# Grouping the first loads of a fused S5 + SwiGLU kernel: twelve transfers in place of fifteen

## The chip, the cores and the metric

The kernel runs on one core of a Trainium2 chip. The metric is the device time of one execution in microseconds (us). Before the change it is 178.52 us, the median of three runs (178.37 to 178.71).

## The reference

A layer norm without gain feeds two branches that are added to the input: a diagonal complex state-space layer (S5) over 2048 tokens, and a SwiGLU feed-forward layer. Width D is 512, the state 512, the hidden width F 1376, everything in bfloat16.

```python
x = A_x                                   # [1, 2048, 512]
xn = _layernorm(x, axis=-1)
return x + _A_ref(xn, ...) + _B_ref(xn, B_w_gate, B_w_up, B_w_down)

def _A_ref(x, ...):                       # S5
    dt = jnp.exp(log_dt)
    Lam_bar = jnp.exp(dt * Lam)
    B_bar = ((Lam_bar - 1.0) / Lam)[:, None] * Bmat
    Bu = jnp.einsum("bld,pd->blp", x + 0j, B_bar)
    # h[t] = Lam_bar * h[t-1] + Bu[t], for t in range(2048)
    return 2.0 * jnp.einsum("blp,dp->bld", hseq, Cmat).real + x * Dskip[None, None, :]

def _B_ref(x, w_gate, w_up, w_down):      # SwiGLU
    return (silu(x @ w_gate) * (x @ w_up)) @ w_down
```

## The kernel before

The 2048 tokens are 16 tiles of 128, and four tiles make a chunk of 512. Most work goes chunk by chunk: B's projection of the normed tokens (`bproj_chunk`, line 380), the rotation and the scans of the recurrence on VectorE (lines 390 to 436), gate and up with their product (`gateup_chunk`, lines 455 to 474), and the output (`out_chunk`), which adds the feed-forward part (line 598) and the state part (line 611) in one PSUM bank. All the order is written out by hand: engines run their instructions in the order of the program, and a backlog of VectorE steps is pumped out between groups of matmuls.

The head is what the change touches. The matrices gate and up arrive row block by row block: row k is the 128 rows of the weight matrix that meet the k-th 128 columns of x, cut to the first 1024 of the 1376 columns (256 KB, `load_row`, line 117). The remaining 352 columns of each come as one transfer into `w_end` (line 113). x comes as tile 0 (SyncE's queue, line 123), tile 1 (ScalarE's queue, line 125), tiles 2 and 3 (lines 131 and 133) and then chunk 1 in one (line 141). SyncE (SP) issues its transfers in the order of the program; at most eight are under way, since each of eight semaphores serves every eighth transfer, and an issue waits for the landing of the transfer that had its semaphore before. A transfer's consumer waits for the whole transfer.

TensorE begins with dummy matmuls (line 668), transposes x of tiles 0 and 1 as soon as they are there (line 230), takes the mean out by a matmul (line 238), and then runs the weight rows in the order in which they arrive, `row_mm` (line 487): up's rows 0 to 3, gate's rows 0 to 2, and gate's row 3, each row with four matmuls (two tiles times two halves of the 1024 columns) into four PSUM banks. Between gate's rows 2 and 3 it transposes tile 2, which VectorE has centered by then:

```python
    row_mm(1, 0)
    pp = prm_transpose()
    ln_stats(2)
    center(2)
    ln_rstd(2, 3)
    ln_stats(3)
    ln_rstd(3, 4)
    prm_copy(pp)
    exp_pool(dt_t[:], ldt)
    for k in range(1, SW):
        row_mm(1, k)
    t2 = bank()
    for k in range(KD):
        cT_mm(t2, xc[:, 2, :], k, k == 0, k == KD - 1)
```

`ln_stats` (lines 182 and 183) are VectorE's statistics, `center` line 219, `ln_rstd` a small addition on VectorE (line 191) and a power on GpSimd (line 192). Tile 3 and then tiles 0 to 2 are normed (line 200) and turned by a DMA transpose (`xT0_dma`, line 251), behind which SP's queue has the transposes of B (line 145). Much later, after chunk 1's gate and up, SP copies A_x of the first three chunks into the output (line 856), and GpSimd adds the results to it with accumulating DMAs (line 618 and line 584).

Of the kernel before, what the change touches and what calls it, by code (L numbers as in the profile page):

```python
# [23 lines left out]
def kernel(  # L24
# [17 lines left out]
    nc = tc.nc  # L42
# [4 lines left out]
    CW = 512  # L47
    HW = CW // 2
    NT = L // 128
    NCH = L // CW  # L50
    TPC = CW // 128
    KD = D // 128
# [27 lines left out]
    x_v = A_x[0].rearrange("(n p) d -> p n d", p=128)  # L80
    out_v = out[0].rearrange("(n p) d -> p n d", p=128)
    wg_v = B_w_gate.rearrange("(k p) f -> p k f", p=128)
    wu_v = B_w_up.rearrange("(k p) f -> p k f", p=128)


    xall = const.tile([128, NT, D], BF16, name="xall")
# [3 lines left out]
    FE = fgroups[-1][0] * 128  # L90
    wg01 = const.tile([128, KD, FE], BF16, name="wg01")
    wu01 = const.tile([128, KD, FE], BF16, name="wu01")
# [18 lines left out]
    def load_w1(q, tiles, view, gi):  # L111
        a, b = fgroups[gi]
        q.dma_start(out=tiles[gi][:, :, :], in_=view[:, :, a * 128:F if gi == len(fgroups) - 1 else b * 128])


    def load_row(q, t, view, k):
        q.dma_start(out=t[:, k, :], in_=view[:, k, 0:FE])

    HK = KD // 2
    ident = const.tile([128, 128], BF16, name="ident")  # L120
# [3 lines left out]
    nc.vector.memset(xall[:, 1, 0:2], 0.0)  # L124
    nc.scalar.dma_start(out=xall[:, 1, :], in_=x_v[:, 1, :])
    nc.scalar.preload_act_table_set("silu_and_others")
    for k in range(KD):
        load_row(nc.sync, wu01, wu_v, k)
    for k in range(HK):
        load_row(nc.sync, wg01, wg_v, k)  # L130
    nc.sync.dma_start(out=xall[:, 2, :], in_=x_v[:, 2, :])
    load_row(nc.sync, wg01, wg_v, HK)
    nc.sync.dma_start(out=xall[:, 3, :], in_=x_v[:, 3, :])
    load_row(nc.sync, wg01, wg_v, HK + 1)
    load_w1(nc.sync, wg_g, wg_v, 2)
    load_w1(nc.sync, wu_g, wu_v, 2)
    prm_rows = const.tile([128, 128], BF16, name="prm_rows")
# [649 lines left out]
    def bproj_chunk(c):  # L787
        need(f"ln{c}")
        for part in range(2):
            for q in range(NQ):  # L790
                bproj_tile(c, part, q)
                pump(BP)
                multiply(0 if q else 1)
# [27 lines left out]
    def queue_ssm(c):  # L821
        fwd, back = ssm_ops(c)
        queue(f"ssm{c}", fwd + back)
# [28 lines left out]
    gateup_chunk(1)  # L852
    nc.gpsimd.dma_start(out=dsk_bc[:], in_=A_Dskip.partition_broadcast(128))
    bproj_chunk(2)
    for a in range(0, (NCH - 1) * CW, CW):
        nc.sync.dma_start(out=out[0, a:a + CW, :], in_=A_x[0, a:a + CW, :])
    queue_ssm(2)
    out_chunk(0)
    gateup_chunk(2)
# [45 lines left out]
```

## Time and profile before

| what | value |
|---|---|
| median of three runs | 178.52 us (178.37 to 178.71) |
| the profiled execution | 177.87 us |
| its span, first to last instruction | 175.8 us |
| TensorE busy | 171.4 us, 97% |
| VectorE busy | 156.9 us, 89% |
| ScalarE busy | 102.0 us, 58% |
| bytes moved by DMA | 17.88 MB, mean 102 GB/s |
| TensorE's granted clock | 0.999 |

Times in a profile's lines are microseconds from the span's start, unless marked ns. In the timeline a line has the start, the time that it took, the engine, the line of the program, the operation, and what it writes from what it reads; "x4" says that four of a kind in a row are one entry. PE is TensorE's matmuls, PEld its weight loads, DVE VectorE, ACT ScalarE, POOL GpSimd, and SPq are instructions of SP's queue, for a DMA the issue alone. In the list of DMAs the last number is the median time from issue to landing. The chain that ended last is followed back from the last instruction, at each step to what released it.

### The profile page before, as it was taken

Reading aid. Unit: us, or ns where it says so; the run is one execution under the profiler, and the core shown is the slowest. Engines: PE = TensorE matmul, PEld = TensorE weight load, DVE = VectorE, ACT = ScalarE, POOL = GpSimd, SP = SyncE. Lnnn points to the kernel's source line nnn. Section 1 sums busy time; section 2 is a strip of 40 time slices with the busy share of each in tenths; the row PEclk is TensorE's granted clock in tenths of the full one; section 3 lists DMA queues with packets and bytes.
Section 4 is the critical chain, followed back from the end, with each engine's and each line's share of the span. In section 5 each row is a group of like instructions: output and inputs, shape, how many; then the busy total and the mean of one; then the engine's idle time right before and its main releaser. Section 6 shows DMA issues by size and latency. Waiting matters only on the chain.

```text
span 175.8 us, 2365 instructions
## 1 busy us (share of the span) xinstructions
PE 171.4 (97%) x847; PEld 82.6 (47%) x863; DVE 156.9 (89%) x259; ACT 102.0 (58%) x188; POOL 28.1 (16%) x39
## 2 busy tenths in 40 slices
PE   8999999999999999999999999999999999999993
PEld 4544446464444444446444444446444444444542
DVE  3776999999999999999999999999999998699542
ACT  3379498793997685236598660024666653990100
POOL 5244110032000000044300000025000000522500
PEclk9999999999999999999999999999999999999999
DMA  5998929999999300047016000007200000696921
GB/s 184 344 350 83 245 48 205 285 191 300 161 218 306 112 4 0 0 38 82 2 34 119 0 0 0 0 0 87 36 15 17 0 4 0 87 175 96 117 66 60
DMA packets 34043, 17.88 MB, mean 102 GB/s; under 512 B 24896, under 2 KB 32928, under 8 KB 33984
## 3 DMA queue, kind: packets, MB, share of 16 engines
q1 hardware_dynamic: 30288, 14.22, 34.1%
q0 software_dynamic: 3456, 3.28, 14.4%
q10 hardware_dynamic: 288, 0.23, 0.4%
q8 instruction: 7, 0.11, 0.3%
q14 instruction: 4, 0.03, 0.1%
HBM read 8.03 MB, written 5.24 MB: 75 GB/s over the span
## 4 chain that ended last, share of the span: by engine, by line
PE 96%; DMA 1%; issue 1%; DVE 0%
PE ps L455 29%; PE ps L598 22%; PE ps L611 16%; PE ps L380 16%; PE ps L487 8%; PE ps L541 3%; PE ps L771 2%; DMA xall<-in_A_x_dram 1%; PE ps L230 1%; PE ps L238 0%; DVE xall L614 0%; PE ps L271 0%
## 5 line engine op out<-in xcount | busy, mean ns | idle before, releaser
L598 PE MATMUL ps<-wd_sb,guT 128*128 128x512 bf16 (+4 forms) x184 | 38.7, 366 | 0.2
L422 DVE TENSOR_TENSOR_SCAN g<-r_t,car,u 128x512 bf16<-128x512 f32 x24 | 29.1, 1264 | 0.0
L611 PE MATMUL ps<-CF,wt 128*128 128x512 bf16 (+2 forms) x134 | 28.4, 366 | 0.1
L380 PE MATMUL ps<-xnT,BT 128*128 128x512 bf16 x125 | 28.1, 379 | 0.2
L598 PEld LDWEIGHTS <-guT 128*128 128x128 bf16 (+1 forms) x187 | 17.9, 98 | 20.5
L455 PE MATMUL ps<-xnT,wu 128*128 128x512 bf16 x95 | 24.6, 379 | 0.2
L455 PE MATMUL ps<-xnT,wg 128*128 128x512 bf16 x91 | 23.9, 379 | 0.1
L618 POOL DMA_DIRECT2D out_dram<-res x12 | 10.5, 1043 | 77.3 <-ACT res L617 72.1
L469 ACT ACTIVATE guT<-ps 128x512 bf16<-128x512 f32 x30 | 18.3, 609 | 4.8 <-PE ps L455 4.5
L470 ACT CAST u<-ps 128x512 bf16<-128x512 f32 x30 | 17.9, 596 | 4.6 <-PE ps L455 4.5
L382 ACT CAST u<-ps 128x512 bf16<-128x512 f32 x32 | 17.5, 597 | 4.8 <-PE ps L380 3.3
L611 PEld LDWEIGHTS <-wt 128*128 128x128 bf16 x136 | 13.0, 98 | 14.7
L380 PEld LDWEIGHTS <-BT 128*128 128x128 bf16 x128 | 12.5, 98 | 14.8
L617 ACT CAST res<-ps 128x512 bf16<-128x512 f32 x12 | 6.8, 583 | 21.0 <-PE ps L611 21.0
L572 ACT ACTIVATE xr<-xall,nb,rstd 128x512 bf16<-128x512 bf16 x16 | 11.8, 805 | 9.1 <-DVE xall L580 4.9
L455 PEld LDWEIGHTS <-wu 128*128 128x128 bf16 x96 | 9.4, 98 | 11.3
L455 PEld LDWEIGHTS <-wg 128*128 128x128 bf16 x96 | 9.3, 98 | 10.6
L192 POOL TENSOR_TENSOR rstd<-ve,neg_half 128x1 f32<-128x1 f32 (+1 forms) x7 | 7.6, 1079 | 29.4 <-DVE ve L191 29.0
L455 PE MATMUL ps<-xnT,w_end 128*128 128x512 bf16 x48 | 10.9, 379 | 0.0
L182 DVE BATCH_NORM_STATS2 stats<-xall 128x6 f32<-128x512 bf16 x16 | 10.8, 675 | 0.0
L474 DVE TENSOR_TENSOR guT<-guT,u 128x1024 bf16<-128x1024 bf16 x15 | 10.0, 675 | 0.0
L390 DVE TENSOR_TENSOR pm<-g,c 128x2048 bf16<-128x2048 bf16 x8 | 9.8, 1220 | 0.1
(120 smaller groups left out, 207.8 us busy)
## 6 DMA issues: line engine op xcount, KB each, us to landing
out_dram<-in_A_x_dram SPq DMA_DIRECT2D x3, 512.0 KB, 5.3
out_dram<-res POOLq DMA_DIRECT2D x12, 128.0 KB, 3.1
out_dram<-xall POOLq DMA_DIRECT2D x3, 512.0 KB, 6.0
wd_sb<-in_B_w_down_dram SPq DMA_DIRECT2D x1, 1280.0 KB, 8.2
wu<-in_B_w_up_dram SPq DMA_DIRECT2D x4, 256.0 KB, 3.8
wg<-in_B_w_gate_dram SPq DMA_DIRECT2D x4, 256.0 KB, 4.8
xall<-in_A_x_dram SPq DMA_DIRECT2D x1, 1024.0 KB, 7.0
xall<-in_A_x_dram SPq DMA_DIRECT2D x1, 512.0 KB, 6.1
```

The costliest lines, as they stand in the source:

```text
L182: nc.vector.bn_stats(out=stats[:, n, 0, :], in_=xall[:, n, :])
L380: nc.tensor.matmul(ps[:] if c else by_k(ps[:]), lhsT=BT[:, part, k, q * 128:(q + 1) * 128], rhs=xnT[:, c, k, :] if c else xnT0[:, k], star ...
L382: nc.scalar.copy(out=u_tiles[c][:, part, q, :], in_=ps[:])
L422: V.tensor_tensor_scan(out=g()[:, part, q, :], data0=r_t[:, q:q + 1].to_broadcast([128, CW]), data1=u_tiles[c][:, part, q, :], initial=ini ...
L455: nc.tensor.matmul(ps[:fs, lo:hi], lhsT=wslice(groups, fi, k), rhs=xnT[:, c, k, lo:hi], start=(k == 0), stop=(k == KD - 1))
L469: nc.scalar.activation(out=guT[:fs, fi, :], in_=psg[:fs], func=ACT.Silu)
L470: nc.scalar.copy(out=u_pair[c][:fs, fi % 2, :], in_=psu[:fs])
L487: nc.tensor.matmul(ps[:, 0:(b - a) * 128], lhsT=tokens(i, k), rhs=groups[gi][:, k, 0:(b - a) * 128], start=(k == 0), stop=(k == KD - 1))
L572: nc.scalar.activation(out=box["xr"][:], in_=xall[:, n, :], func=ACT.Identity, scale=rstd[:, n:n + 1], bias=nb[:, n:n + 1])
L598: nc.tensor.matmul(o[:], lhsT=gu_tiles[c][:fsz[fi], fi, i * 128:(i + 1) * 128], rhs=wd_sb[:fsz[fi], fi, lo:hi], start=(fi == 0), stop=False)
L611: nc.tensor.matmul(o[:], lhsT=w_tiles[c][:, part, q, i * 128:(i + 1) * 128], rhs=CF[:, part, q, lo:hi], start=False, stop=(part == 1 and q ...
L618: nc.gpsimd.dma_start(out=out_v[:, n, lo:hi], in_=res[:, lo:hi], accum_op=ALU.add)
```

## The change

The three loads of rows are grouped: up's rows 2 and 3 come in one transfer, gate's rows 0 and 1 in one, and x of tiles 2 and 3 in one, which stands behind gate's row 2 where x of tile 2 stood ahead of it. `load_row` becomes `load_rows` with a range of rows. Transfers before the end weights: x of tile 0, x of tile 1, up 0, up 1, up 2 and 3, gate 0 and 1, gate 2, x of tiles 2 and 3, gate 3. In the same edit the copies of A_x into the output become six of 256 rows in place of three of 512. No instruction of TensorE, VectorE, ScalarE or GpSimd is added, removed or moved; what changes is which landing they wait for.

```diff
-    def load_row(q, t, view, k):
-        q.dma_start(out=t[:, k, :], in_=view[:, k, 0:FE])
+    def load_rows(q, t, view, k0, k1):
+        q.dma_start(out=t[:, k0:k1, :], in_=view[:, k0:k1, 0:FE])
...
-    for k in range(KD):
-        load_row(nc.sync, wu01, wu_v, k)
-    for k in range(HK):
-        load_row(nc.sync, wg01, wg_v, k)
-    nc.sync.dma_start(out=xall[:, 2, :], in_=x_v[:, 2, :])
-    load_row(nc.sync, wg01, wg_v, HK)
-    nc.sync.dma_start(out=xall[:, 3, :], in_=x_v[:, 3, :])
-    load_row(nc.sync, wg01, wg_v, HK + 1)
+    for k0, k1 in ((0, 1), (1, 2), (2, KD)):
+        load_rows(nc.sync, wu01, wu_v, k0, k1)
+    load_rows(nc.sync, wg01, wg_v, 0, 2)
+    load_rows(nc.sync, wg01, wg_v, 2, 3)
+    nc.sync.dma_start(out=xall[:, 2:TPC, :], in_=x_v[:, 2:TPC, :])
+    load_rows(nc.sync, wg01, wg_v, 3, KD)
     load_w1(nc.sync, wg_g, wg_v, 2)
     load_w1(nc.sync, wu_g, wu_v, 2)
...
-    for a in range(0, (NCH - 1) * CW, CW):
-        nc.sync.dma_start(out=out[0, a:a + CW, :], in_=A_x[0, a:a + CW, :])
+    for a in range(0, (NCH - 1) * CW, HW):
+        nc.sync.dma_start(out=out[0, a:a + HW, :], in_=A_x[0, a:a + HW, :])
```

KD is 4, TPC is 4, HK is 2, CW is 512 and HW is 256.

## The prediction

> **What bounds the kernel now.** I read the page's busy times first, then the chain that ended last, then the timeline and the DMA landings of the first 13 us, because the change lies there.
>
> ```profile
> span 175.8 us, 2365 instructions
> PE 171.4 (97%) x847; PEld 82.6 (47%) x863; DVE 156.9 (89%) x259; ACT 102.0 (58%) x188; POOL 28.1 (16%) x39
> ...
> PE 96%; DMA 1%; issue 1%; DVE 0%
> ```
>
> TensorE is busy 97% of the span and makes 96% of the chain. In order of time the chain has one DMA piece, the first x tile, and then only TensorE with gaps of 0.05 us:
>
> ```profile
> 0.74 2.48 DMA xall<-in_A_x_dram
> ...
> 5.14 4.32 PE ps L487 x20
> 9.46 0.06 PE ps L271
> 9.51 1.08 PE ps L487 x5
> ...
> 11.24 0.22 PE ps L230 x4
> 11.46 4.32 PE ps L487 x20
> ```
>
> So there is no later idle time in which a late TensorE could catch up: what it loses in the head arrives whole at the end. From 5 us it runs up's four weight rows, then gate's. 20 matmuls take 4.32 us, 0.216 each, and a row has four: 0.865 us a row. What the rows and the change's x tiles are needed for:
>
> ```profile
> 4.98 3.62 PE L487 MATMUL ps<-wu,CF 128*128 128x512 bf16 x16
> 8.43 1.03 PE L487 MATMUL ps<-wg,CF 128*128 128x512 bf16 x4
> 8.98 0.69 DVE L182 BATCH_NORM_STATS2 stats<-xall 128x6 f32<-128x512 bf16 x1
> 9.71 0.18 DVE L183 BATCH_NORM_AGGREGATE mv<-stats 128x2 f32<-128x6 f32 x1
> 9.92 0.35 DVE L219 TENSOR_SCALAR CF<-xall,mv 128x512 bf16<-128x512 bf16 x1
> 10.86 0.42 PEld L230 LDWEIGHTS <-CF 128*128 128x128 bf16 x4
> ```
>
> Up's row 2 is needed at 4.98 + 8 x 0.216 = 6.71 and row 3 at 7.57; gate's row 0 at 8.43 and row 1 at 9.35. When they land follows from SP's issues and the time from issue to landing:
>
> ```profile
> 1.19 1.84 SPq L117 DMA_DIRECT2D wu<-in_B_w_up_dram  x4
> ...
> 7.02 0.38 SPq L113 DMA_DIRECT2D w_end<-in_B_w_up_dram  x1
> ```
>
> ```profile
> wu<-in_B_w_up_dram SPq DMA_DIRECT2D x1, 256.0 KB, 4.0
> ...
> wu<-in_B_w_up_dram SPq DMA_DIRECT2D x1, 256.0 KB, 4.4
> ```
>
> The four issues start 0.47 us apart. Row 2, the third, lands at 2.12 + 4.0 = 6.1 and row 3 at 2.60 + 4.4 = 7.0; the issue at 7.02 waits for just that landing and confirms it. By the same sums row 0 lands at 4.2, row 1 at 5.25, gate's rows 0 and 1 at 7.8 and 8.35, x of tile 2 at 8.7, gate's row 2 at 9.4, x of tile 3 at 9.73, gate's row 3 at 10.5. The table of stretches shows the DMA engines 90 to 107% busy in each of the nine microseconds from 2 to 11, so the order of bytes, not the issue, sets these times.
>
> **The change part by part.** *Up's rows 2 and 3 together.* Row 2's first matmul now waits for the pair. The pair's last byte is row 3's last byte, in the same place of the stream: 7.0. With 0.04 us from landing to start (x of tile 0 lands at 3.22, the first engine starts at 3.24, TensorE at 3.27) row 2 starts at 7.04 instead of 6.71: a stall of **0.33 to 0.34 us** where there was none. Behind it on TensorE stands everything, up to the last matmul. Row 3 follows without its own wait. Bounds: if the pair were complete when row 2 was (6.1), the stall is 0; it can't be below, since TensorE has no idle time to give back. If both rows move as slowly as row 1 did (5.25 - 4.19 = 1.06 us), the pair lands at 5.25 + 2.12 = 7.37: 0.70 us. I take 0.34, the row it is nearest to.
>
> Here a rule of the Trainium skill ("DMA: Bandwidth & Descriptors", section Bandwidth) can be weighed: bigger transfers run closer to peak, and its measured table has 64 KB at 138 GB/s and 1 MB at 341. The rows here say 256 KB in about 0.85 us from 5.25 to 7.0, some 300 GB/s, already with other transfers queued behind. By the page the pair would land earlier than 7.0 and the stall shrink towards 0, by the rows it is 0.34; this is the second rival below.
>
> *Gate's rows 0 and 1 together.* The pair lands with row 1, 8.35; it is needed at 8.43 + 0.34 = 8.77. Cost 0; the stall before it is the cover, and without it 0.08 us would be left.
>
> *x of tiles 2 and 3 together, behind gate's row 2.* Row 2 of gate moves 128 KB forward (9.4 to about 9.05) and is needed above 10.2: nothing. Tile 2's x moves from 8.7 to 9.73, where tile 3's was. VectorE's statistics of tile 2 then start at 9.75 instead of 8.98, and centering ends after 0.69 + 0.04 + 0.18 + 0.03 + 0.35 = 1.29 us more, at 11.04 instead of 10.27. TensorE loads it for the transposes at 10.86, or at 11.20 with the stall ahead of it: covered by 0.1 us. If the stall were 0, this would cost about 0.2 us by itself (bounds 0 and 0.2), so it is not added to the 0.34 but lies under it.
>
> VectorE and, through the row sums' power (L192) and the index table, GpSimd run about 0.77 us late from here on; VectorE is nearly gapless afterwards, so it stays late. What waits for it: the transpose of tile 3 lands at 14.9 + 0.8, needed at 18.0; B's real part, behind the transposes on SP's queue (12.45 and 13.84, then 15.17), lands at 21.3 + 0.8 = 22.1 and is needed at 22.3 + 0.34, the tightest, 0.5 us; chunk 1's transpose lands at 29.3 + 0.8, needed at 31.0; the last C factor is ready at 72.56 + 0.8, needed at 74.2 + 0.34. Cost 0, and up to 0.8 us less those margins should one go.
>
> *SP's queue.* Three issues fewer of 0.47 us each: the later loads are issued up to 2 us earlier, but the DMA engines are full until 13. Nor does a smaller number of transfers move the same bytes sooner: gate's row 2 took 0.68 us of the stream, the two x tiles of half its size 0.36 and 0.33. Gain 0.
>
> *The copies of A_x into out* (not in the heading, but in the diff) become six of 256 KB. Three more issues of about 0.59 us (2.27 for three now, the first 1.02) lie on SP between 54.5 and its next use at 88.22. The same bytes land by about 60 (59.8 now); GpSimd's first accumulating store waits for ScalarE until 75.49. Cost 0, cover 15 us; without cover 1.8 us.
>
> Sum: +0.34. The profiled execution took 177.87, 2.07 outside its span, and is 0.65 below the median; so 178.21 for it, and on the median 178.52 + 0.34 = **178.86**.
>
> **The rivals.**
> 1. *The forecast:* one stall at up's row 2, 0.2 to 0.6 us, 178.72 to 179.12. A change of this kernel can be told from none at about 0.2%, 0.36 us, so this case straddles the bound.
> 2. *The bigger transfer moves faster.* The last head load, 512 KB, lands 1.3 us after the transfer before it (12.6 to 13.9), so two rows could take 1.3 instead of 1.75: the pair lands at 5.25 + 1.3 = 6.55, before 6.71, the x pair some 0.4 us earlier too (9.3, centering done at 10.6 before 10.86), and nothing waits. 178.5. Against it: those packets came at a time with nothing else in the queues, the early rows did not.
> 3. *Landings later than in this one profile.* The timed runs are 0.5 to 0.84 us longer than the profiled one. Before, row 3 may land 0.5 us late and costs nothing (7.57 against 7.0); after, each tenth is paid: 0.34 + 0.5 = 0.84, 179.36. It decides from 0.1 us of lateness on; an x pair landing after 9.85 does the same at the transposes.
> 4. *Faster.* If part of those 0.65 us is TensorE waiting in the timed runs for gate's row 3 or the end weights, whose issues wait for earlier landings (5.70, 6.19, 7.02), then issuing them 1.5 to 2 us earlier takes it back: at most 0.65 less the 0.34, 178.2. It needs gate's row 3 to land after 11.4 instead of 10.5; nothing in the profile shows that.
>
> **How the numbers follow.** Forecast 0.55, of it 0.34 above the bound and 0.21 below; rival 2 0.18, no change; rival 3 0.18, slower; rival 4 0.09, faster. Slower 0.52, same 0.39, faster 0.09. The range leaves out the outer half of rival 4 and of rival 3: 178.40 to 179.35; the forecast's own is 178.72 to 179.12.
>
> **What would show it.** Right: in the profile after, the 16 up matmuls are split by an idle of about 0.34 us before the ninth, released by the up transfer; the rest of the chain is as before, 0.34 later; VectorE's statistics of tile 2 start near 9.75. Wrong: no idle there (rival 2), an idle above 0.6 us or a second one at the transposes of tile 2 or at B's real part (rival 3), or an idle of TensorE in the profile before that I took for none.

## The result, and the profile after

The changed kernel takes 180.00 us (median of six runs, 179.63 to 180.83), the kernel before 178.50 us beside it (six runs, 178.14 to 178.71). The ratio is 1.0088, 95% interval 1.0063 to 1.0113: 1.5 us slower, and outside the range that was given. The profiled execution took 179.9 us, with a span of 177.6.

The page of the changed kernel, its span, its busy times and the shares of the chain that ended last:

```profile
span 177.6 us, 2369 instructions
...
PE 172.1 (97%) x847; PEld 82.6 (46%) x863; DVE 156.9 (88%) x259; ACT 100.9 (57%) x188; POOL 28.6 (16%) x39
...
PE 66%; DVE 17%; DMA 7%; ACT 4%; POOL 2%; SPq 1%; issue 1%; DVEq 0%
```

TensorE still looks 97% busy, since 1 us of idling in 177 hides in the rounding. The chain tells more: TensorE had 96% of it before and has 66% now. The timeline of its head shows why (start, duration, engine, line; in brackets the idle time before and what ended it):

```profile
4.92 1.25 PE L485 MATMUL ps<-wu,CF 128*128 128x512 bf16 x4
...
6.50 1.02 PE L485 MATMUL ps<-wu,CF 128*128 128x512 bf16 x4 [0.33 <-DMA wu<-in_B_w_up_dram]
...
8.16 1.89 PE L485 MATMUL ps<-wu,CF 128*128 128x512 bf16 x8 [0.64 <-DMA wu<-in_B_w_up_dram]
...
9.88 1.03 PE L485 MATMUL ps<-wg,CF 128*128 128x512 bf16 x4
...
10.91 0.69 DVE L180 BATCH_NORM_STATS2 stats<-xall 128x6 f32<-128x512 bf16 x1 [1.86 <-DMA xall<-in_A_x_dram]
11.86 0.35 DVE L217 TENSOR_SCALAR CF<-xall,mv 128x512 bf16<-128x512 bf16 x1
...
12.32 0.42 PEld L228 LDWEIGHTS <-CF 128*128 128x128 bf16 x4
```

Up's sixteen matmuls, one unbroken piece of 3.62 us before, fall into three pieces. The idle time before the ninth is 0.64 us, and there is another of 0.33 before the fifth. The second row starts at 6.50, after row 1's landing at 6.46; the third, which needs the pair, at 8.16. Gate's row 0 starts at 9.88 instead of 8.43: 1.45 us are lost here. The DMA issues of the changed kernel give the pair's landing (KB, then median us from issue to landing):

```profile
wu<-in_B_w_up_dram SPq DMA_DIRECT2D x1, 512.0 KB, 6.0
```

Issued at 2.12, it landed at 8.12, where row 3 had landed at 7.00. The stretches of the head show the DMA engines at work meanwhile; the last two columns are DMA share and GB/s. Before:

```profile
4.00:5.00 1.00, 1.00 (x11) 0.89 (x9) 0.36 (x3) 0.27 (x1) 0.00 (x0) 1.00 1.05 296
5.00:6.00 1.00, 1.00 (x6) 0.44 (x5) 0.82 (x4) 0.60 (x3) 0.00 (x0) 1.00 1.03 331
```

After:

```profile
4.00:5.00 1.00, 1.00 (x10) 0.88 (x9) 0.31 (x3) 0.30 (x2) 0.00 (x0) 1.00 0.70 136
5.00:6.00 1.00, 1.00 (x5) 0.38 (x4) 0.84 (x4) 0.55 (x3) 0.00 (x0) 1.00 0.74 257
```

From 4 to 6 us about 390 KB moved instead of 630. And there is a second, smaller loss. The chain of the changed kernel, in order of time, begins with the x pair and VectorE and comes back to TensorE at the transposed x of chunk 2:

```profile
3.62 7.26 DMA xall<-in_A_x_dram
...
10.91 0.71 DVE stats L180
...
53.60 4.32 DMA xnT<-xn
57.92 0.05 issue
57.96 5.14 PE ps L378 x23
```

These matmuls began at 56.24 before. With the 1.45 us of the head they would have begun at 57.69, so 0.27 us are added there, and TensorE ends 1.73 us after its end in the profile of before.

What held chunk 2's transposition back was its place in SP's queue. ScalarE had normed the last tile of chunk 2 by 51.92 (the line of the timeline starts at 51.07 and takes 0.85), but SP had two transposes of C (`CT`) and one of a gate tile to issue first:

```profile
42.07 6.84 SPq L842 DMA_TRANSPOSE CT<-in_A_C_re_dram  x1
48.95 3.19 SPq L842 DMA_TRANSPOSE CT<-in_A_C_im_dram  x1
52.31 1.19 SPq L548 DMA_TRANSPOSE guT<-g_last  x1
53.60 1.34 SPq L253 DMA_TRANSPOSE xnT<-xn  x1
```

Before, the first of these four issues started at 39.49 and the last at 50.28.

The 1.73 us of these two traces are not the 1.5 us of the medians taken apart. The profile of before was of a quick execution (177.87 against a median of 178.5), so the typical loss inside the span is smaller; and the time outside the span grew. In the six runs of the changed kernel it is 2.29 to 2.43 us, median 2.32. In the executions of before that were timed beside the experiments it is 1.89 to 2.17, median about 2.04. So some 0.3 of the 1.5 us lies outside the span, where no profile shows it, and about 1.2 inside it.

### The profile page after: what moved, and what is told of

Read it like the earlier page. It is cut to its first block, busy times and chain, and to the rows that moved or that the text cites. A ratio compares the mean times of both kernels' runs of the same rounds, so it can differ in the third digit from the quotient of the medians.

```text
span 177.6 us, 2369 instructions
## 1 busy us (share of the span) xinstructions
PE 172.1 (97%) x847; PEld 82.6 (46%) x863; DVE 156.9 (88%) x259; ACT 100.9 (57%) x188; POOL 28.6 (16%) x39
## 4 chain that ended last, share of the span: by engine, by line
PE 66%; DVE 17%; DMA 7%; ACT 4%; POOL 2%; SPq 1%; issue 1%; DVEq 0%
PE ps L596 21%; PE ps L453 19%; PE ps L609 16%; PE ps L378 8%; DMA xall<-in_A_x_dram 4%; DVE stats L180 3%; DVE pm L301 3%; DMA xnT<-xn 2%; DVE pm L388 2%; ACT xn L203 2%; DVE pm L300 2%; ACT guT L467 2%; PE ps L539 1%; DVE guT L520 1%; SPq L117 1%
## 5 line engine op out<-in xcount | busy, mean ns | idle before, releaser
L616 POOL DMA_DIRECT2D out_dram<-res x12 | 10.5, 1042 | 77.1 <-ACT res L615 70.7
```

The costliest lines, as they stand in the source:

```text
L616: nc.gpsimd.dma_start(out=out_v[:, n, lo:hi], in_=res[:, lo:hi], accum_op=ALU.add)
```

## The experiments

The twenty profiles are easiest to read together. "Landed" is the last of the sixteen semaphore increments of a transfer, one from each DMA engine, in us from the start of the span; the start of gate's row 0 on TensorE sums up what the head lost until then (8.43 in the profile of before). These columns are of one execution each. The column "median start" says how typical it is, and is an estimate: from gate's row 0 to TensorE's last matmul it is 164.70 us in sixteen of the twenty profiles (0.04 to 0.43 more in e3, k2, after and g2, which have the x pair), so the median span of a kernel's timed runs, less what follows gate's row 0 in its profile, gives the start in a typical run, to about 0.1 us and to 0.4 in kernels with the x pair. The last column is the ratio of times to the kernel before on the same chip.

| kernel | row 1 landed | row 2 | row 3 | pair | gate's row 0 starts | median start | ratio |
|---|---|---|---|---|---|---|---|
| before (profile) | 5.29 | 6.17 | 7.00 | | 8.43 | | |
| f4, before again | 5.31 | 6.02 | 6.63 | | 7.93 | 8.6 | 0.9990 |
| e2, gate pair alone | 6.20 | 6.84 | 7.45 | | 8.86 | 8.8 | 1.0005 |
| e3, x pair alone | 6.33 | 6.93 | 7.57 | | 8.96 | 9.0 | 1.0026 |
| e4, copies alone | 6.25 | 6.90 | 7.51 | | 8.88 | 8.8 | 1.0029 |
| f3, row 2 held to 2.82 | 5.78 | 6.94 | 7.70 | | 8.71 | 8.8 | 1.0005 |
| g1, no parameter loads | 5.85 | 6.58 | 7.23 | | 8.47 | 8.7 | 1.0016 |
| g4, row 3 on ScalarE's queue | 6.21 | 6.83 | 6.03 | | 9.07 | 9.2 | 1.0027 |
| h4, row 1 on ScalarE's queue | 5.34 | 5.77 | 6.54 | | 8.10 | 9.0 | 1.0000 |
| k1, rows 2 and 3 in halves | 5.86 | 6.57 | 7.39 | | 9.31 | 9.3 | 1.0062 |
| k2, the change but up's pair | 5.75 | 6.45 | 7.06 | | 8.66 | 8.9 | 1.0051 |
| after | 6.46 | | | 8.12 | 9.88 | 9.9 | 1.0088 |
| e1, up's pair alone | 6.89 | | | 8.22 | 9.99 | 9.7 | 1.0057 |
| f1, the change but the copies | 6.99 | | | 8.29 | 10.06 | 10.0 | 1.0081 |
| f2, pair held to 2.82 | 6.58 | | | 8.18 | 9.95 | 9.8 | 1.0054 |
| g2, after, no parameter loads | 6.84 | | | 8.14 | 9.90 | 9.8 | 1.0072 |
| g3, pair held to 3.26 | 5.18 | | | 8.18 | 9.94 | 9.3 | 1.0040 |
| h1, pair in two halves | 6.15 | | | 7.13, 8.61 | 10.47 | 10.5 | 1.0096 |
| h2, pair on ScalarE's queue | 7.28 | | | 7.48 | 9.91 | 9.9 | 1.0056 |
| h3, nothing behind the pair | 5.33 | | | 7.77 | 9.53 | 9.3 | 1.0035 |

Two things stand out. The pair as one transfer on SP's queue, with gate's loads right behind it, lands within 8.12 to 8.29 in all six profiles, and gate's row 0 then starts within 9.88 to 10.06. With single rows everything varies by a microsecond and more. The narrow range is partly chance, though: the profiled executions of e1 and g3 are the longest of their runs, and by the medians g3 starts gate's row 0 at 9.3, half a microsecond ahead of the other five.

### The parts one by one

Up's rows 2 and 3 grouped, nothing else:

```diff
-    for k in range(KD):
-        load_row(nc.sync, wu01, wu_v, k)
+    for k0, k1 in ((0, 1), (1, 2), (2, 4)):
+        load_rows(nc.sync, wu01, wu_v, k0, k1)
```

> Before with only up's rows 2 and 3 in one transfer; gate, x and the copies as before. In the profile of the whole change row 1 of up, which is not grouped, landed at 6.46 instead of 5.29 and the pair at 8.12 instead of 7.00, and the DMA engines were only 70 and 74% busy from 4 to 6 us. Theory A (crowding: the more is issued right behind row 1, the thinner row 1's own stream): the up pair is issued at 2.12, next behind row 1, so this part alone gives most of it, row 1 after 6.0, the pair after 7.6, and 1.0 to 1.5 us on the time, 179.5 to 180.0. Theory B (only the pair's own two-row pattern is slow): row 1 lands near 5.3 as before, the pair at 7.5 to 8.1, and the time is 0.8 to 1.4 longer. Theory C (the forecast's mechanism alone, with the rest coming from the other parts): row 1 at 5.3, pair at 7.0, +0.34, 178.85.

Measured: 179.26 against 178.38, ratio 1.0057 (1.0038 to 1.0077), 1.0 us. The landings are those of theory A, the time lies below its range. TensorE's part of the timeline:

```profile
4.48 1.03 PE L487 MATMUL ps<-wu,CF 128*128 128x512 bf16 x4
6.93 1.02 PE L487 MATMUL ps<-wu,CF 128*128 128x512 bf16 x4 [1.42 <-DMA wu<-in_B_w_up_dram]
8.27 1.89 PE L487 MATMUL ps<-wu,CF 128*128 128x512 bf16 x8 [0.31 <-DMA wu<-in_B_w_up_dram]
9.99 1.03 PE L487 MATMUL ps<-wg,CF 128*128 128x512 bf16 x4
```

The idle time ahead of the pair is only 0.31 here, yet its row starts at 8.27 as in the whole change: TensorE had already lost its time to row 1. The pair's landing sets the start, not the sum of the stalls ahead of it. So this part carries about two thirds of the loss of 1.5 us.

Gate's rows 0 and 1 grouped, nothing else:

```diff
-    for k in range(HK):
-        load_row(nc.sync, wg01, wg_v, k)
+    load_rows(nc.sync, wg01, wg_v, 0, 2)
```

> Before with only gate's rows 0 and 1 in one transfer. Theory A: its issue at 3.07 falls while rows 1 to 3 of up move; row 1 is hardly touched, rows 2 and 3 land 0.3 to 0.8 later, so the time is 0 to 0.5 us longer (row 3 has 0.57 of slack). Theory B: up's rows as before, the gate pair lands at 8.8 to 9.3 instead of 8.35 and is needed at 8.43: +0.4 to 0.9 us. Forecast's mechanism: the pair lands at 8.35, +0, 178.5.

Measured: 178.31, ratio 1.0005 (0.9986 to 1.0024). The pair landed at 8.82, where gate's row 1 alone landed at 8.93 (e3) and 8.88 (e4). This is the forecast's own mechanism: it costs nothing, and 512 KB in one transfer keep their place in the stream here, 1.4 us after the transfer ahead of them.

x of tiles 2 and 3 grouped, nothing else:

```diff
-    nc.sync.dma_start(out=xall[:, 2, :], in_=x_v[:, 2, :])
     load_row(nc.sync, wg01, wg_v, HK)
-    nc.sync.dma_start(out=xall[:, 3, :], in_=x_v[:, 3, :])
+    nc.sync.dma_start(out=xall[:, 2:TPC, :], in_=x_v[:, 2:TPC, :])
     load_row(nc.sync, wg01, wg_v, HK + 1)
```

> Before with only the x tiles 2 and 3 in one transfer behind gate's row 2. All theories: rows of up as before. x lands at 9.75, VectorE's statistics of tile 2 start near 9.75 and centering ends at 11.04, while TensorE wants it at 10.86: +0.1 to 0.25 us, 178.6 to 178.75. VectorE is 0.8 us later after that, which nothing should wait for.

Measured: 178.81, ratio 1.0026 (1.0004 to 1.0049), 0.46 us with a wide interval. The trace accounts for 0.2 of it: the x pair landed at 10.36, tile 2's transposes started 0.14 us late, and some 0.05 us came at 98 us. Another 0.05 is the closing, which the next experiment explains.

The copies of A_x as six, nothing else:

```diff
-    for a in range(0, (NCH - 1) * CW, CW):
-        nc.sync.dma_start(out=out[0, a:a + CW, :], in_=A_x[0, a:a + CW, :])
+    for a in range(0, (NCH - 1) * CW, HW):
+        nc.sync.dma_start(out=out[0, a:a + HW, :], in_=A_x[0, a:a + HW, :])
```

> Before with only the copies of A_x into the output made six of 256 rows. All theories: no difference, within 0.2 us of 178.5; the copies land by about 61, GpSimd's first store waits for ScalarE at 75.5. If they cost something, it must show as TensorE idle near 56 us, where chunk 2's transposed x is waited for.

Measured: 178.84, ratio 1.0029 (1.0008 to 1.0050), 0.5 us, where at most 0.2 was expected. Nothing on TensorE answers to it between the head and the last matmul. The time lies after the last store. The last lines of the timeline of this kernel:

```profile
core 0 of [0], span 176.6 us
...
173.62 0.29 DVE L614 TENSOR_TENSOR xall<-ps,xall 128x128 bf16<-128x128 f32 x1 [0.51 <-PE ps L611]
173.94 0.33 SPq L615 DMA_DIRECT2D out_dram<-xall  x1
```

And of the changed kernel:

```profile
core 0 of [0], span 177.6 us
...
174.90 0.29 DVE L612 TENSOR_TENSOR xall<-ps,xall 128x128 bf16<-128x128 f32 x1 [0.51 <-PE ps L609]
175.22 0.33 SPq L613 DMA_DIRECT2D out_dram<-xall  x1
```

From the issue of the last store to the end are 2.69 us here (span 176.63) and 2.38 there (177.60). The store itself takes 1.43 to 1.47 us in all the profiles; the rest is SP's closing series of waits, one after another and 0.06 us apart in the trace, one for each semaphore. Whichever semaphore the last store happens to have decides how many waits are still to come. The trace has 40 transfers on SP's and ScalarE's queues before, and 0.92 us from the last landing to the end; with 39 it is 0.97 or 0.98 (seven profiles), with 37 1.09, with 41 1.34, with 42 1.29, with 43 (this kernel) 1.23: it goes round with the count modulo eight. All the profiles with 40 have 0.90 to 0.92. The change takes three loads away and adds three copies, 40 again, and so pays nothing here. Of e4's 0.5 us, 0.31 are this. Another 0.18 lie outside the span (median 2.22 us against 2.04), so nothing is left for the copies' work itself.

The whole change with the copies left at three:

> The whole change without the six copies: they stay three of 512 rows. The copies alone gave a ratio of 1.0029 (interval 1.0008 to 1.0050) with nothing in TensorE's order of events to show for it. If they truly cost 0.3 to 0.5 us, this kernel is 1.1 us over before, ratio 1.006; if that was the spread of the head, it is as the whole change, 1.3 to 1.7 us over before, ratio 1.0075 to 1.0095. Head: row 1 of up at 6.2 to 6.9, the pair 1.25 to 1.7 later.

Measured: 179.69, ratio 1.0081 (1.0054 to 1.0108), or 1.44 us, of which 0.17 us is the closing (37 transfers); the time outside the span is 2.04, as before. That leaves 1.3 us inside the span, and the changed kernel has 1.2, so there the six copies are no part of the loss. Whether the 0.3 us outside the span come with them is not shown: e4 and k2, which have the six copies, have 0.18 and 0.29 more outside it, but g2, which has them too, has 2.08, and g1, which has three, 2.20.

### Is it crowding?

The first theory was that the pair is late because transfers crowd in the queue. Two kernels hold the third transfer back to 2.82 us with a two-column write of ScalarE into its tile, once with the pair, once with single rows:

```diff
+    nc.scalar.copy(out=wu01[:, 2, 0:2], in_=ident[:, 0:2])
```

> Up's pair alone, but its issue is held back from 2.12 to about 2.8 us by a two-column write of ScalarE into the pair's place, so that row 1 has the queue to itself for longer. Theory A (crowding by what is issued right behind row 1): row 1 lands earlier than in the pair alone (6.89 there), at 6.2 or before, the pair 1.25 after it, and the time falls from 179.26 to 178.6 to 178.9. Theory B (the pair's own pattern, or a pair simply being waited for whole, whatever is crowded): the pair lands no earlier than 7.5, and the time stays at 179.1 to 179.6 or grows by the delay.

> Before, ungrouped, with the issue of row 2 held back from 2.12 to about 2.8 us in the same way. Theory A: row 1's late landing (6.2 to 6.3 in three looks, 5.29 in the one profile of before) is made by the rows issued behind it too; it lands at 5.3 to 5.7, rows 2 and 3 at 6.2 and 7.0, and the time falls to 177.7 to 178.1. If the late row 1 has another cause (the small parameter loads of GpSimd, the start of the stream), it stays at 6.2 and the time at 178.4 or a little above.

Measured: 179.31, ratio 1.0054 (1.0034 to 1.0073), pair at 8.18; and 178.24, ratio 1.0005 (0.9993 to 1.0017), rows at 6.94 and 7.70. Issuing 0.7 us later moves the pair's landing by nothing. With single rows, row 1 landed at 5.78 and the time is 178.24, between the two expectations.

The kernel before once more, to see how far two profiles of one kernel differ:

> The kernel before, unchanged, as a null: how far two medians of the same kernel lie apart here, and where up's row 1 lands in a second look. Ratio 1.000, interval over 1; a median within 0.25 us of the other. If row 1 lands near 6.2, the profile of before was a lucky execution (5.29) and before's typical execution already stalls there by 0.4 to 0.5; if near 5.3, the late row 1 belongs to the changed kernels.

Measured: 178.05, ratio 0.9990 (0.9973 to 1.0007). Its profiled execution took 177.37, with row 3 0.4 us earlier still than in the profile of before.

The second theory was that GpSimd's three small parameter loads, issued at 1.78 to 3.02 among the weight rows, disturb the stream. Both kernels without them (constants of -0.5 in their place):

```diff
-    nc.gpsimd.memset(prm_rows[:], 0.0)
-    for i, v in enumerate((A_Lambda_re, A_Lambda_im, A_log_dt)):
-        nc.gpsimd.dma_start(out=prm_rows[i * NQ:(i + 1) * NQ, :], in_=v.rearrange("(q j) -> q j", j=128))
+    nc.gpsimd.memset(prm_rows[:], -0.5)
```

> Before without GpSimd's three small parameter loads (Lambda and log_dt; the parameters are set to the constant -0.5 instead, so the state layer is computed with other parameters). In every look so far the stream of the weight rows is thin between 3.3 and 6.3 us, with packets of 2 KB that take 250 to 1200 ns instead of 84, and these loads move just then (4.1 to 7.3 and later). Theory P (the parameter loads thin the stream): long packets nearly gone, row 1 of up lands at 5.3 or before in every execution, time 177.4 to 177.9 with a small spread. Theory Q (the stream starts thin by itself): row 1 anywhere from 5.3 to 6.3, time 178.0 to 178.4 with the old spread of about 1 us.

> The whole change, without the same three loads. Theory P: row 1 at 5.3, the pair at 6.6 to 7.0, so only the forecast's stall of 0.3 to 0.4 us (and x's late centering under it) is left: 177.8 to 178.4, that is 0.3 to 0.5 over the ungrouped kernel without the loads. Theory Q: row 1 at 6.4 to 7.0 and the pair at 8.1 to 8.3 as with the loads, 179.4 to 180.0.

Measured: 178.31, ratio 1.0016 (0.9991 to 1.0041), and 179.56, ratio 1.0072 (1.0040 to 1.0104), pair at 8.14. This theory falls. g2 has the second loss of the changed kernel again; its timeline:

```profile
58.13 2.12 PE L376 MATMUL ps<-xnT,BT 128*128 128x512 bf16 x9 [0.26 <-DMA xnT<-xn]
```

The pair held until x of tile 0 has landed (the write above, from `xall`, so that the issue starts at 3.26):

> Up's pair alone, its issue held until x of tile 0 has landed (about 3.4 us instead of 2.12). Held to 2.82 it did not get row 1 in early (6.58). If what stands in the queue behind row 1 matters at all, row 1 now lands at 5.3 to 5.8 as in the ungrouped kernels that had luck, the pair at 7.0 to 7.6, and the time is 178.6 to 179.1. If row 1 is late whatever stands behind it, it lands at 6.2 to 7.0, the pair at 8.0 to 8.5, and the time is 179.2 to 179.7.

Measured: 178.84, ratio 1.0040 (1.0024 to 1.0057). Row 1 now lands on time, at 5.18, and in this profile the pair at 8.18 all the same, so here it is not row 1 that delays the pair. But the profiled execution, 179.44, is the longest of nine. By the median, gate's row 0 starts at 9.3, which puts the pair's landing at about 7.5, and the time is the one expected if the queue behind row 1 matters. So holding the pair to 3.26 gains some 0.4 us on e1, though the intervals of the two ratios overlap.

Single rows, row 3 on ScalarE's queue at 1.30, ahead of its turn:

```diff
+    load_row(nc.scalar, wu01, wu_v, KD - 1)
...
-    for k in range(KD):
+    for k in range(KD - 1):
         load_row(nc.sync, wu01, wu_v, k)
```

> Before, ungrouped, with up's row 3 issued on ScalarE's queue at about 1.3 us instead of the fourth on SyncE's at 2.60. As many bytes are then asked for behind row 1 as with the pair, and earlier, but in transfers of one row. If it is the crowd of bytes that makes row 1 late, row 1 lands at 6.5 to 7.0 and the time is 178.8 to 179.4. If it is the transfer of two rows itself, row 1 lands at 5.3 to 6.3 as before, a little later for sharing the engines with row 3 (two rows in 1.3 us), time 178.2 to 178.8.

Measured: 178.72, ratio 1.0027 (1.0001 to 1.0052). As many bytes as the pair, early and on two queues: rows at 6.03, 6.21 and 6.83, within what was expected if it is the two rows in one transfer.

### What about the pair is slow?

Four kernels take its properties apart. In two halves of 64 partitions, each as long as a row:

```diff
-    for k in range(KD):
+    for k in range(HK):
         load_row(nc.sync, wu01, wu_v, k)
+    for p0 in (0, 64):
+        nc.sync.dma_start(out=wu01[p0:p0 + 64, 2:4, :], in_=wu_v[p0:p0 + 64, 2:4, 0:FE])
```

> Up's rows 2 and 3 grouped, but as two transfers of 64 partitions with both rows each, issued in the places of row 2 and row 3; the rest as before. If the length of one transfer is what makes the pair late, each half is as long as a row, the halves land near 6.9 and 7.4, the stall ahead of row 2 is that of a pair that lands with row 3 (at most 0.7 us), and the time is 178.5 to 178.8. If it is the pattern of two rows for a partition, the last half lands at 8.1 to 8.3 like the pair, and the time is 179.2 or more.

Measured: 179.99, ratio 1.0096 (1.0062 to 1.0129), as slow as the whole change. The timeline of TensorE:

```profile
4.68 1.03 PE L489 MATMUL ps<-wu,CF 128*128 128x512 bf16 x4
...
6.19 1.02 PE L489 MATMUL ps<-wu,CF 128*128 128x512 bf16 x4 [0.49 <-DMA wu<-in_B_w_up_dram]
...
8.75 1.89 PE L489 MATMUL ps<-wu,CF 128*128 128x512 bf16 x8 [1.53 <-DMA wu<-in_B_w_up_dram]
```

The length of one transfer is not it. The halves landed at 7.13 and 8.61. Its control has the same 64 partitions and one row each:

```diff
-    for k in range(KD):
+    for k in range(HK):
         load_row(nc.sync, wu01, wu_v, k)
+    for k in range(HK, KD):
+        for p0 in (0, 64):
+            nc.sync.dma_start(out=wu01[p0:p0 + 64, k, :], in_=wu_v[p0:p0 + 64, k, 0:FE])
```

> Up's rows 2 and 3 each as two transfers of 64 partitions, so four transfers of 128 KB with one row each in the place of the two of 256 KB. It shares with the two halves of the pair the 64 partitions and more issues, and lacks only the two rows for a partition. If the halves of the pair were late for their two rows, these land like whole rows: the last by 6.6 to 7.7, row 2's by 6.0 to 7.0, time 178.0 to 178.6. If it is the 64 partitions or the further issues, row 2 lands past 7.0 and row 3 past 8, time 179.0 or more.

Measured: row 2 complete at 6.57, row 3 at 7.39, as whole rows. By these landings it is the two rows for each partition in one transfer that is late at this place. The time does not say so as clearly: 179.13, ratio 1.0062 (1.0045 to 1.0078), was expected at 178.0 to 178.6 and missed. 0.37 us of it is the closing (42 transfers); no idle time stands in TensorE's head, but a group that is too long:

```profile
4.98 4.49 PE L490 MATMUL ps<-wu,CF 128*128 128x512 bf16 x16
```

This led to the third finding. The same group, asked for by tile (count; duration min, median, max in ns), before:

```profile
L487 PE MATMUL ps<-wu,CF x16: 379/379/380, 5.0 to 8.2; 128*128 128x512 bf16 x16
```

In the changed kernel, and in k1:

```profile
L485 PE MATMUL ps<-wu,CF x16: 376/378/604, 4.9 to 9.7; 128*128 128x512 bf16 x16
```

```profile
L490 PE MATMUL ps<-wu,CF x16: 379/379/634, 5.0 to 9.1; 128*128 128x512 bf16 x16
```

Some matmuls take 604 to 634 ns, and these start 0.43 us after one another instead of 0.216: TensorE still runs at half rate when up's rows begin, four matmuls long in k1, one in the changed kernel, none in the profile of before. The granted clock is 1.00 in all these stretches, so that column does not show it. Over the 20 profiles the turn to the full rate comes anywhere from about 3.5 us (g3) to 6.8 (k1), and the half rate lengthens up's rows by 0 to 1.0 us: in k1 by 0.87, in h3 by 0.98. The Trainium skill ("TensorE: Matmul & The Clock Gate", section Part 1: The HAM clock gate) states such a gate, with half rate until a free-running window of activity has been filled, so that the turn shifts from execution to execution, and 426.7 against 215.7 ns for 512 columns; the starts here agree with both.

That the half rate explains k1's median is not shown, though. The spans of its nine runs are 176.9 to 177.5, none of them far below the profiled 177.1, where a cost that changes from execution to execution should leave some runs quick. Measured by the median starts, before is at 8.6, k1 at 9.3 and h1 at 10.5: so transfers of 64 partitions cost something too, for a reason that stays open, and the two rows cost more.

The pair on ScalarE's queue at 1.30, rows 0 and 1 on SP's:

```diff
+    load_rows(nc.scalar, wu01, wu_v, 2, KD)
...
-    for k in range(KD):
-        load_row(nc.sync, wu01, wu_v, k)
+    for k0, k1 in ((0, 1), (1, 2)):
+        load_rows(nc.sync, wu01, wu_v, k0, k1)
```

> Up's pair alone is grouped, and issued on ScalarE's queue at about 1.3 us instead of on SP's at 2.12; rows 0 and 1 stay on SP. If the pair needs a fixed time from its issue or from its turn in SP's queue, it lands by 7.4, row 1 perhaps at 6.5, and the time is 178.4 to 178.9. If the stream of 3 to 6 us is thin whenever a transfer of two rows stands in it, the pair lands at 8.1 to 8.3 again and the time is 179.2 or more.

Measured: 179.42, ratio 1.0056 (1.0036 to 1.0075). The landing is near the first expectation, the time in the second. The pair landed at 7.48, 6.18 us after its issue, as long as when it is issued at 2.12 with gate's loads behind it (6.0 to 6.2); that this is no fixed time, f2 and g3 show (5.36 and 4.92). Its bytes came in front of the others: row 0 landed at 5.28, row 1 at 7.28, and gate's row 0 started at 9.91 because TensorE wants rows 0 and 1 first. All four rows were there at 7.48, as with single rows (row 3 at 6.63 to 7.57), and the transfer rate was the usual one (344 and 369 GB/s from 5 to 7 us), so a transfer of two rows does not thin the stream wherever it stands.

The pair at 2.12, with gate's loads behind it held until x of tile 0 has landed (ScalarE writes two columns of gate's tile first):

```diff
+    nc.scalar.copy(out=wg01[:, 0, 0:2], in_=xall[:, 0, 0:2])
```

> Up's pair is grouped and issued at 2.12 as in the change, but gate's row 0 and with it all that stands behind it on SP's queue is held until x of tile 0 has landed, about 3.3 us (ScalarE writes two columns of the tile first). If the transfers issued behind the pair take the stream from it, the pair lands by 7.4 and the time is 178.5 to 178.8. If the pair is slow by itself, it lands at 8.1 to 8.3 and the time is 179.2 or more.

Measured: 178.80, ratio 1.0035 (1.0020 to 1.0049). Its landing, 7.77, is between the two expectations, the time at the upper end of the first; row 1 is on time (5.33), so the pair right behind row 1 need not make it late:

```profile
4.68 2.87 PE L488 MATMUL ps<-wu,CF 128*128 128x512 bf16 x8
7.81 1.89 PE L488 MATMUL ps<-wu,CF 128*128 128x512 bf16 x8 [0.26 <-DMA wu<-in_B_w_up_dram]
```

The first group here has 2.87 us for eight matmuls where the second has 1.89: the half rate again. What is issued behind the pair takes some 0.4 us from it, by the profile and by the median starts (9.3 against 9.7 in e1), and the rest of its lateness remains with nothing behind it until 3.1 us.

### Can row 1 be had earlier, and what is left without up's pair?

```diff
+    load_row(nc.scalar, wu01, wu_v, 1)
...
-    for k in range(KD):
+    for k in (0, 2, 3):
```

> Nothing is grouped; up's row 1 is issued on ScalarE's queue at about 1.3 us instead of second on SP's. Row 1 landed at 5.2 to 6.3 us in the looks at ungrouped kernels and is needed at 5.84. If its late landings are what the executions of before lose, it lands by 5.3 in this form and the time is 177.5 to 178.0, faster than both kernels. If an earlier issue changes nothing in the order of the bytes, it lands near 6 and the time stays 178.2.

Measured: 178.53, ratio 1.0000 (0.9977 to 1.0023). In the profile row 1 landed at 5.34 and no time was lost (177.48, the quickest of the runs), but the median is a microsecond longer. No gain: one early row 1 does not settle the spread, to which the half rate belongs as well. None of the kernels beats the one before.

The whole change with up's rows left single:

```diff
-    for k0, k1 in ((0, 1), (1, 2), (2, KD)):
+    for k0, k1 in ((0, 1), (1, 2), (2, 3), (3, KD)):
```

> The whole change but up's rows 2 and 3, which stay two transfers. If up's pair carries most of the change's loss, up's row 2 lands by 7.0 and row 3 by 7.7, the x pair may cost TensorE 0 to 0.3 us, and the time is 178.3 to 179.0, ratio 1.001 to 1.004. If the losses of the other parts alone (0.26 and 0.29%) were real and add up, it is 179.1 to 179.3, ratio 1.005 to 1.006.

Measured: 179.07, ratio 1.0051 (1.0030 to 1.0072), 0.9 us. The trace has the x pair at 9.85, no stall at tile 2's transposes and none at chunk 2's transposed x, but 41 transfers and so 0.42 us more of closing than in the changed kernel. Another 0.29 us lie outside the span, as in the changed kernel. Some 0.2 us (-0.2 to 0.6) remain inside the span for everything but up's pair. So the 1.5 us are about 0.3 outside the span, 0.2 for the rest of the change and 1.0 for up's pair, as in e1.

## Why the prediction was wrong

*What held.* TensorE's order bounds the kernel, and what the head loses arrives at the end: 1.45 us are gone at gate's row 0 and still at the last matmul. Row 2 waits for the pair, and the idle time lies before the ninth matmul. Gate's pair costs nothing. The copies' transfers delay nothing inside the span. Fewer issues on SP's queue gain nothing: the end weights are issued at 5.77 and 6.39, 0.4 and 0.6 us earlier, and nothing came sooner. Tile 2's centering, done at 12.21, still reached TensorE's load at 12.32, covered by the 0.1 us that was worked out. This was luck, since VectorE was 1.9 us late and TensorE 1.45, where 0.77 and 0.34 were forecast. Where the pair of up was not there to give that cover (e3), 0.14 us were paid, near the 0.2 that the text gave.

*The step that failed* is "The pair's last byte is row 3's last byte, in the same place of the stream: 7.0". The pair landed at 8.12 in the profile after and at 8.12 to 8.29 in all six profiles; in the typical run of the four kernels below it landed at about 8.1. That is past 7.37 too, the upper end that took both rows to move as slowly as row 1 (7.49 with row 1's landing as the trace has it, 5.29 and not 5.25). The sum took single rows' landings as a property of the bytes' place in the stream; up to 8 us they are not. The first of the sixteen engines is through with the pair at 5.8 to 6.4 us, about when the first is through with row 3 of single rows (5.8 to 6.2), but the last is 1.8 to 2.4 us behind the first, for row 3 0.8 to 1.5 us (1.8 in f3). A transfer lands with its slowest engine.

*One profile as the typical one.* "Needed at 6.71" and "row 3 at 7.0" are from an execution without half rate in up's rows and with row 1 on time. In the seven profiles whose up rows are four loads on SP as before and not held (before, f4, e2, e3, e4, g1, k2), row 3 lands at 7.21 and row 2 starts at 6.87 in the mean, worked out as 1.73 us before gate's row 0. With 0.04 from landing to start, the stall would be 0.38: both values moved together, and the predicted term would have survived. So this did not cause the miss. It explains part of the 0.65 us between the profiled execution and the median, though: gate's row 0 starts 0.17 us later in the mean of the seven, to which later landings and, what rival 3 left out, the half rate both add.

*The stall against the loss.* With the pair at 8.2, gate's row 0 starts at 9.96 in the mean of the four profiles with the pair at 2.12 on SP and the usual loads behind (after, e1, f1, g2), and at 8.60 in those seven: 1.36 us instead of 0.34. By the median starts it is 9.9 against 8.8, 1.0 us, which agrees with e1's time. Because the start is set by the landing alone, an execution that is late before (row 1, half rate) pays less idle time ahead of the pair, and a quick one more.

*VectorE's lateness.* The x pair was put at 9.73 and landed at 10.88, the statistics of tile 2 started at 10.91, 1.9 us late and not 0.77. "Cost 0, and up to 0.8 us less those margins" then failed at a place that the prediction had not listed, the transposed x of chunk 2: 0.27 us in the changed kernel, 0.43 in g2, none in f1 and k2. VectorE's lateness alone does not decide it. In f1 VectorE was as late (statistics of tile 2 at 11.08), but SP's issue of the second transpose of C took 2.18 us, not 3.19 as in the changed kernel or 3.80 as in g2, so chunk 2's transposition was issued at 52.35 and came in time. Why that issue varies is open.

*The rivals.* The second, that the bigger transfer moves faster, is refuted: no profile has the pair before 7.48. Of the rule of the Trainium skill that bigger transfers run closer to peak ("DMA: Bandwidth & Descriptors", section Bandwidth), these runs show nothing at this place; the measurement decides, and says that 512 KB as one transfer land about 1 us later than as two. The table there is of transfers that GpSimd issues, and these are issued by SP. The third rival came nearest in size (179.36), and the idle of 0.64 us is just past the 0.6 named as its sign, but by a lateness that the grouping itself brings and not one that was there before. The fourth, a gain from earlier issue, is refuted by e2 and k2.

*What stays open.* Why a transfer with two rows for each partition is late at this place. It isn't its length (h1), an issue at 2.12 rather than 2.82 (f2), or the parameter loads (g2). An issue at 3.26 (g3) and an empty queue behind it (h3) each take away some 0.4 us of about 1.0, not all. On ScalarE's queue it came at the usual rate (h2), and behind other transfers, as gate's pair, it costs nothing (e2). That it is the two rows for each partition rests on the landings of h1 and k1, one profile each; their timed runs agree with their profiles (spans 177.5 to 178.5 and 176.9 to 177.5), but k1's are late as well. A pattern with two rows that lie together in memory was not tried.

## What to carry to other kernels

A grouped transfer need not land where its last part landed: a consumer that took the parts one by one waits for the slowest of sixteen engines on all of it, and in the first microseconds, where nothing is buffered yet, that was about 1 us here, three times the wait that the order of bytes gave. Group loads that are consumed late and leave the first ones single. And before a landing or a need is taken from one profile, read a second profile of the same kernel, and the spans of its timed runs: here the two profiles differ by half a microsecond, more than the effect that was predicted.

## What the runs showed of the hardware

- Early in the stream, 10 to 38 packets of 2 KB in each profile take 250 to 1600 ns, where the median is 84 to 87, most of them starting from 3.3 to 7 us, in kernels with and without the pair. In the changed kernel the DMA engines also stand partly idle in that time: a DMA share of 0.70 and 0.74 from 4 to 6 us where it was 1.05 and 1.03.
- TensorE's half rate lengthens the first real matmuls by 0 to 1.0 us, another amount in each execution, while the granted clock reads 1.00. It shows only in the starts and in the largest duration of a group.
- The end of a kernel depends on the number of its transfers: 0.90 to 1.34 us from the last landing to the end, in steps of 0.06 us, by which of the eight semaphores the last store has. An edit that changes the number of transfers by one can cost 0.42 us without touching anything else, as in k2.
- The time outside the span depends on the program too: 2.0 to 2.1 us in the median of most kernels here, 2.2 to 2.3 in four (the changed kernel, e4, k2 and g1), for a reason that stays open.
